# Attention with a feed-forward block: the last pass's token tiles are normalised on VectorE instead of GpSimd, and two of its operand chunks get earlier due times

## The chip, the cores and the metric

The kernel runs on one core of a Trainium2 chip. The metric is the device time of one execution in microseconds (us); three runs of the kernel before gave 906.70, 906.96 and 907.29, so the median is 906.96. In the texts TensorE is also called PE, VectorE DVE, ScalarE ACT and GpSimd POOL; SP issues the DMAs.

## The reference

Four batches, 12 heads, 448 positions, head size 64, all float32. After attention the heads are put side by side (1792 tokens of 768 features), normalised over the features, and sent through a two-layer block without a residual of the normalised value:

```
scores = cap * tanh(scale * q @ k.T / cap)
attn   = softmax(scores)                 # with + 1e-9 under the sum
x      = (attn @ v), heads side by side  # 4 x 448 x 768
mu, var = mean and variance of x over the 768 features
xn  = (x - mu) / sqrt(var + 1e-6) * g_ln
out = x + relu(xn @ w_ch1) @ w_ch2       # 768 -> 3072 -> 768
```

## The kernel before

**Tiling.** The 1792 tokens are 14 tiles of 128 (x(0) to x(13)). They are handled in four groups (GROUPS): A0 (tiles 0 to 2), A1 (3 to 5), C0 (6 to 9) and C1 (10 to 13). The 3072 hidden features are 24 blocks of 128 (FC); each block has a slice of w1 and a slice of w2. Every product is made in float32 precision from operands split into a high and a low part, as three matmuls (high by high, high by low, low by high). The split is one ACT instruction that rounds (helper `round`, L398) and one DVE instruction that takes the rest (helper `rest`, L405).

**Stages.** Attention comes first, four heads at a time (`quad`), with the group A work woven between. For A0 and A1 the FFN goes block by block (`ffn`): `up` (L883 to L885) makes the hidden values of a block in a PSUM bank, `bend` (L894 on ACT, L896 on DVE) applies relu and splits them, `down` (L912 to L914) multiplies with w2 into another bank, and a DVE add (L917) takes that bank into x. `up` and `down` share the eight PSUM banks with all else, and a bank is used again only when what it held has been read.

**The last pass.** C0 and C1 are handled last, 512 tokens each, with a seven-product scheme over 2 x 2 blocks (`last`, `stage`; matmuls L1048 to L1051). `blocks` (L927 on) prepares its operands, while the `up` and `down` work of A0 and A1 still runs. It loads the eight tiles of C0 and C1 (SP, `load_x`, L993), computes mean and reciprocal deviation in `mv` (`statistics`: DVE, with one power on POOL, L737), and normalises each tile in place, `x = (x - mean) * rstd` (L939, one instruction per tile of 128 x 768). Then, for each of KH = 3 feature chunks c, it transposes four 512-column pieces on PE (L959, four transposes of 128 x 128 in a row, one from each tile of the group), copies them out on ACT with the gain (L963, to a buffer y), forms three differences on DVE (L972) and splits the seven operands X (L398 on ACT, L405 on DVE, 128 x 512). A transpose of the group C0 needs tiles 6 to 9, one of C1 tiles 10 to 13; the instructions of PE stand in a fixed order, so a transpose that waits holds all that follows it.

**Order.** The order of each engine is made before the run by a planner (`Order.emit`): it plays the program in time with a cost for each operation and, when an engine is free, takes the ready operation that is due first. The costs are formulas: `POOL1(DM) + 61` (1006 for a tile) for L939 on POOL, `VEC1(DM) + 61` (697) for the same form on DVE in `norm` (L756). The due time of chunk c is `begin + c * PLAN["chunk"]`. The chip then runs each engine's list in that order, each instruction waiting for its semaphores.

Of the kernel before, what the change touches and what calls it, by code (L numbers as in the profile page):

```python
# [18 lines left out]
DM, DFF = H * D, 4 * H * D  # L19
# [20 lines left out]
VEC1 = lambda n: 60 + 0.75 * n  # L40
# [3 lines left out]
POOL1 = lambda n: 100 + 1.1 * n  # L44
# [27 lines left out]
PLAN = dict(  # L72
    qk=8000, pre=16000, pv=-2000, fin=9000, early=26000, start=108000, step=16700, spread=0.85, late=18,
    w1=20000, w2=3000, evac=2000, bstep=6300, cstep=31200, cnorm=10000, load=20000, zpad=3000, rush=30000, ahead=20000,
    again=12000, down=16000, chunk=12000, blocks=-30000,
)

KINDS = dict(
# [5 lines left out]
    e=('e', 3), ot=('b', 4), ss=('b', 1), stage=('a', 3),  # L84
# [9 lines left out]
    e=('e', 2), t=('e', 2), ot=('b', 3), ss=('b', 1), stage=('a', 1),  # L94
# [31 lines left out]
class Order:  # L126
# [8 lines left out]
    def add(self, engines, fn, reads=(), writes=(), allocs=(), due=0.0, dma=0, after=()):  # L135
        op = Op()
        (op.engine, op.cost), = engines.items()
        op.fn, op.due, op.dma, op.seq = fn, due, dma, len(self.ops)
        deps = set(after)
        for k in reads:  # L140
            deps.update(self.writer.get(k, ()))
        for k in writes:
            deps.update(self.writer.get(k, ()))
            deps.update(self.readers.get(k, ()))
        for k in writes:
            self.writer[k], self.readers[k] = [op], []
        for k in reads:
            self.readers.setdefault(k, []).append(op)
        deps.discard(op)
        op.left, op.outs, op.ready, op.end, op.wait, op.after = len(deps), [], 0.0, None, None, deps  # L150
        for d in deps:
            d.outs.append(op)
        bufs = {k[0] if isinstance(k, tuple) else k: 0 for k in (*reads, *writes, *allocs)}
        op.bufs = [b for b in bufs if isinstance(b, Buf)]
        for b in op.bufs:
            b.users += 1
            op.ready = max(op.ready, b.since)
        self.ops.append(op)
        return op
# [168 lines left out]
class Program:  # L328
# [25 lines left out]
    def buf(self, pool, tag, shape, dtype, bufs=1):  # L354
        size = 1
        for x in shape[1:]:
            size *= x
        kinds, tags = (GENERAL_KINDS, GENERAL_TAGS) if self.general else (KINDS, TAGS)
        if tag in tags:
            kind, n = tags[tag]  # L360
            self.limits[pool, tag] = n
            bufs, size = kinds[kind]
        else:
            kind = tag
        self.places[pool, kind] = bufs
        b = Buf(pool, kind, tag, shape, dtype)
        self.sizes[pool, kind] = max(size, self.sizes.get((pool, kind), 0))
        return b
# [558 lines left out]
    def blocks(self, due):  # L927

        nc, add, buf = self.nc, self.add, self.buf
        mvs = []
        for key in ("C0", "C1"):
            t0, nt = GROUPS[key]
            for tl in range(t0, t0 + nt):
                self.load_x(tl, due, [self.gate])
            mv = self.statistics(key, due)
            for m, tl in enumerate(range(t0, t0 + nt)):
                add({"G": POOL1(DM) + 61}, lambda e, tl=tl, mv=mv, m=m: nc.gpsimd.tensor_scalar(  # L939
                    self.x(tl), self.x(tl), mv.ap[:, m, 0:1], mv.ap[:, m, 2:3], op0=ALU.subtract, op1=ALU.mult),  # L940
                    reads=[mv], writes=[self.xkey(tl)], due=due)
        T = self.T = {}
        for c in range(KH):
            for n, name in enumerate(("11", "22", "3", "1", "2", "21", "4")):
                home = "xo1" if 7 * c + n < EARLIER else "xo2"
                T[name, c] = buf(home, f"X{name}{c}", [128, 2, TOK], F32R, 1)
        begin = due
        for c in range(KH):
            due = begin + c * PLAN["chunk"]

            def turned(y, j, n, more=(), after=()):
                key = ("C0", "C1")[n]
                t0, nt = GROUPS[key]
                ps = buf("ps", "tp", [128, 512], F32)
                k = j * KH + c

                def turn(e):
                    for m in range(nt):
                        nc.tensor.transpose(ps.ap[:, m * 128:(m + 1) * 128], self.x(t0 + m)[:, k * 128:(k + 1) * 128], self.ident)  # L959

                first = add({"T": 109 * nt}, turn, reads=[self.xkey(t0 + m) for m in range(nt)], writes=[ps],
                            allocs=[y, *more], due=due, after=after)
                add({"A": ACTP(TOK) + 93}, lambda e: nc.scalar.activation(y.ap, ps.ap, AF.Copy, scale=self.gt[:, k:k + 1]),  # L963
                    reads=[ps], writes=[y], due=due)
                return first

            def keep(name, y):
                t = T[name, c]
                self.split(Part(t, 0), Part(t, 1), y, due, n=TOK)

            def less(out, a, b):
                add({"V": VEC2(TOK)}, lambda e: nc.vector.tensor_tensor(out=out.ap, in0=a.ap, in1=b.ap, op=ALU.subtract),  # L972
                    reads=[a, b], writes=[out], due=due)

            b11, b12, b22, t3, b21 = (buf("y", "y", [128, TOK], F32) for _ in range(5))
            first = [turned(b11, 0, 0, (b12, b22, t3))]
            keep("11", b11)
            turned(b12, 0, 1, after=first)
            turned(b22, 1, 1, after=first)
            keep("22", b22)  # L980
            less(t3, b22, b12)
            keep("3", t3)
            less(b12, b12, b11)
            keep("1", b12)
            less(b22, b22, b12)
            keep("2", b22)
            turned(b21, 1, 0, after=first)
            keep("21", b21)
            less(b21, b21, b22)
            keep("4", b21)  # L990
# [256 lines left out]
```

## Time and profile before

| | us |
|---|---|
| median of three runs | 906.96 (906.70 to 907.29) |
| the profiled execution | 906.14 |
| its span, first to last instruction | 904.3 |
| PE busy | 880.2 (97% of the span) |
| DVE busy | 628.1 (69%) |
| ACT busy | 405.3 (45%) |
| POOL busy | 102.6 (11%) |
| DMA share (16 engines) | 41.9% on the main queue |

The profile is one execution recorded by the hardware. "Busy" is the time an engine spends in instructions; what is left on PE is waits. 906.14 is 1.84 above the span, for what lies around the first and last instruction. A row of the timeline shows start, length, engine, line, operation, output and input, and in brackets the idle time ahead of it with what ended it. The granted clock is the share of full speed that TensorE's throttle allowed.

### The profile page before, as it was taken

How to read it: one execution, taken by the hardware profiler on the slowest of the kernel's cores; microseconds unless marked ns; L12 is line 12 of the kernel's file. 1: busy time of each engine (PE TensorE's matmuls, PEld its weight loads, DVE VectorE, ACT ScalarE, POOL GpSimd, SP SyncE). 2: the span in 40 equal slices, each digit the busy share in tenths (PEclk: the TensorE clock that was granted, in tenths of full speed). 3: DMA queues.
4: the chain of work that ended last, by engine and by line, in shares of the span. 5: the costliest groups of instructions: out<-in, count | busy, mean ns of one | idle time of the engine just before them, and what ended most of it. 6: DMA issues, size and time to landing. Idle time of an engine off the chain costs nothing.

```text
span 904.3 us, 12584 instructions
## 1 busy us (share of the span) xinstructions
PE 880.2 (97%) x4802; PEld 727.0 (80%) x4802; DVE 628.1 (69%) x1056; ACT 405.3 (45%) x630; POOL 102.6 (11%) x122
## 2 busy tenths in 40 slices
PE   9899999999999999999969999999999999999997
PEld 4334577969878888797959889988998999899887
DVE  2995687868887777768729967665666666566544
ACT  7889746463565464643225633233223223312310
POOL 1430131111120111101380000000000000000000
PEclk9999999999999999999979999999999999999999
DMA  9995436585675655545713173111211212120004
GB/s 228 258 252 152 128 117 189 160 254 160 198 216 179 196 154 201 165 137 158 269 49 138 56 278 90 50 56 50 70 36 36 71 36 70 36 70 18 1 1 144
DMA packets 43478, 115.90 MB, mean 128 GB/s; under 512 B 6033, under 2 KB 18833, under 8 KB 43409
## 3 DMA queue, kind: packets, MB, share of 16 engines
q1 hardware_dynamic: 43408, 115.00, 41.9%
q8 instruction: 40, 0.66, 0.3%
q14 instruction: 30, 0.24, 0.1%
HBM read 87.46 MB, written 27.53 MB: 127 GB/s over the span
## 4 chain that ended last, share of the span: by engine, by line
PE 89%; DVE 3%; POOL 3%; ACT 2%; DMA 1%; issue 1%; POOLq 0%; SPq 0%; DVEq 0%; ACTq 0%
PE bank L912 13%; PE bank L914 12%; PE bank L913 12%; PE bank L1048 7%; PE bank L1051 6%; PE bank L1049 6%; PE bank L604 5%; PE bank L883 5%; PE bank L450 5%; PE bank L885 5%; PE bank L884 5%; POOL x L939 2%; PE bank L532 1%; PE bank L572 1%; PE bank L620 1%; PE bank L457 1%
## 5 line engine op out<-in xcount | busy, mean ns | idle before, releaser
L917 DVE TENSOR_TENSOR x<-bank,x 128x384 f32<-128x384 f32 x336 | 182.5, 552 | 76.7 <-PE bank L914 76.0
L912 PE MATMUL bank<-w,hh 128*128 128x384 f32 x672 | 227.9, 339 | 0.0
L914 PE MATMUL bank<-w,hl 128*128 128x384 f32 x672 | 226.8, 338 | 0.0
L913 PE MATMUL bank<-w,hh 128*128 128x384 f32 x672 | 226.8, 338 | 0.0
L912 PEld LDWEIGHTS bank<-w,hh 128*128 128x128 f32 x672 | 126.6, 188 | 5.9 <-issue 2.7
L913 PEld LDWEIGHTS bank<-w,hh 128*128 128x128 f32 x672 | 126.6, 188 | 0.6
L914 PEld LDWEIGHTS bank<-w,hl 128*128 128x128 f32 x672 | 126.6, 188 | 0.0
L1048 PE MATMUL bank<-X,q 128*128 128x512 f32 x252 | 99.7, 396 | 1.4 <-ACT y L1058 1.4
L883 PE MATMUL bank<-hA,q 128*128 128x384 f32 x288 | 100.7, 350 | 0.1
L1049 PE MATMUL bank<-X,q 128*128 128x512 f32 x252 | 99.6, 395 | 0.0
L1051 PE MATMUL bank<-X,q 128*128 128x512 f32 x252 | 99.6, 395 | 0.0
L885 PE MATMUL bank<-hA,q 128*128 128x384 f32 x288 | 98.1, 341 | 1.1 <-DVE q L405 1.1
L884 PE MATMUL bank<-lA,q 128*128 128x384 f32 x288 | 98.2, 341 | 0.0
L638 ACT ACTIVATE e<-bank,sc 128x448 f32<-128x448 f32 x144 | 81.8, 662 | 27.5 <-PE bank L604 27.4
L398 ACT ACTIVATE w<-c 128x768 fp32r<-128x768 f32 x35 | 29.0, 843 | 122.3 <-issue 78.4
L814 POOL TENSOR_SCALAR raw<-raw 128x768 f32<-128x768 f32 x48 | 51.3, 1071 | 230.2 <-ACT c L810 221.2
L405 DVE TENSOR_TENSOR q<-c,q 128x384 fp32r<-128x384 f32 (+1 forms) x88 | 60.3, 687 | 21.2 <-ACT q L398 20.6
L896 DVE SCALAR_TENSOR_TENSOR hl<-bank,hh 128x384 fp32r<-128x384 f32 (+1 forms) x60 | 34.7, 579 | 52.2 <-ACT hh L894 52.0
L398 ACT ACTIVATE q<-c 128x384 fp32r<-128x384 f32 (+1 forms) x84 | 50.2, 604 | 46.0 <-DVE c L819 16.2
L642 ACT ACTIVATE e<-e,capt 128x1344 f32<-128x1344 f32 x48 | 66.6, 1454 | 0.0
L604 PE MATMUL bank<-d 64*128 64x448 f32 x288 | 65.2, 564 | 0.6 <-DVE x L582 0.4
L894 ACT ACTIVATE hh<-bank 128x384 fp32r<-128x384 f32 (+1 forms) x60 | 30.7, 512 | 77.0 <-PE bank L885 60.7
(103 smaller groups left out, 1144.3 us busy)
## 6 DMA issues: line engine op xcount, KB each, us to landing
raw<-in_w_dram SPq DMA_DIRECT2D x48, 768.0 KB, 5.0
kept<-c SPq DMA_DIRECT2D x47, 384.0 KB, 5.6
c<-kept SPq DMA_DIRECT2D x29, 384.0 KB, 3.8
d<-in_kq_dram SPq DMA_DIRECT2D x48, 224.0 KB, 6.3
d<-kept SPq DMA_DIRECT2D x27, 384.0 KB, 3.6
x<-xd SPq DMA_DIRECT2D x16, 384.0 KB, 6.3
v<-in_v_dram SPq DMA_DIRECT2D x24, 227.5 KB, 5.3
out_dram<-x SPq DMA_DIRECT2D x28, 192.0 KB, 1.9
```

The source lines that it names most:

```text
L604: self.nc.tensor.matmul(z[k].ap[:, :S], lhsT=kqs[p].ap[rows[k], l, 128 * j:128 * j + 128], rhs=kqs[p].ap[rows[k], r], start=True, stop=True)
L638: add({"A": ACTP(S) + 93}, lambda e: nc.scalar.activation(tiles[p].ap[:, k, j] if p < 2 else er.ap[:, k], z.ap[:, :S], AF.Tanh, scale=self ...
L883: nc.tensor.matmul(ps.ap[:, :n], lhsT=w1h.ap[:, wc], rhs=xh.ap[:, c], start=(c == 0), stop=False)
L884: nc.tensor.matmul(ps.ap[:, :n], lhsT=w1h.ap[:, wc], rhs=xl.ap[:, c], start=False, stop=False)
L885: nc.tensor.matmul(ps.ap[:, :n], lhsT=w1l.ap[:, wc], rhs=xh.ap[:, c], start=False, stop=(c == CC - 1))
L912: nc.tensor.matmul(o, lhsT=h[0].ap[:, mc], rhs=w[0].ap[:, hc], start=(f == 0), stop=False)
L913: nc.tensor.matmul(o, lhsT=h[0].ap[:, mc], rhs=w[1].ap[:, hc], start=False, stop=False)
L914: nc.tensor.matmul(o, lhsT=h[1].ap[:, mc], rhs=w[0].ap[:, hc], start=False, stop=(f == last))
L917: add({"V": VEC2(HALF)}, lambda e, t=t, ps=ps, hc=hc: nc.vector.tensor_tensor(out=self.x(t)[:, hc], in0=ps.ap[:, :HALF], in1=self.x(t)[:, ...
L1048: nc.tensor.matmul(ps.ap, lhsT=wh.ap[:, wc], rhs=xs[c].ap[:, 0], start=start and c == 0, **o)
L1049: nc.tensor.matmul(ps.ap, lhsT=wh.ap[:, wc], rhs=xs[c].ap[:, 1], start=False, **o)
L1051: nc.tensor.matmul(ps.ap, lhsT=wl.ap[:, wc], rhs=xs[c].ap[:, 0], start=False, **o)
```

## The change

Two lines differ. The eight in-place normalisations of `blocks` (L939) are given to DVE, with the cost formula that `norm` uses; and PLAN["chunk"] goes from 12000 to 8000, so chunk 1 is due 4000 and chunk 2 is due 8000 planner units sooner.

```
-    again=12000, down=16000, chunk=12000, blocks=-30000,
+    again=12000, down=16000, chunk=8000, blocks=-30000,
...
-                add({"G": POOL1(DM) + 61}, lambda e, tl=tl, mv=mv, m=m: nc.gpsimd.tensor_scalar(
+                add({"V": VEC1(DM) + 61}, lambda e, tl=tl, mv=mv, m=m: nc.vector.tensor_scalar(
                     self.x(tl), self.x(tl), mv.ap[:, m, 0:1], mv.ap[:, m, 2:3], op0=ALU.subtract, op1=ALU.mult),
```

On DVE, where the statistics of C1 have just ended (L733), the eight normalisations are set between evictions of `down` banks (L917), the last steps of a weight conversion (L819, L405) and the relu rests (L896). mv_651 is the statistics tile of C0, mv_989 that of C1, x_3532 the tile that holds C0 and C1, x_433 and x_418 those of A1 and A0.

```order
 L917 TENSOR_TENSOR x_433<-bank_275,x_433 128x384
+L819 SCALAR_TENSOR_TENSOR d_75<-d_75,raw_272 128x768
 L917 TENSOR_TENSOR x_433<-bank_254,x_433 128x384
+L939 TENSOR_SCALAR x_3532<-x_3532,mv_651 128x768
+L939 TENSOR_SCALAR x_3532<-x_3532,mv_989 128x768
 L405 TENSOR_TENSOR w_69<-d_75,w_69 128x768
+L939 TENSOR_SCALAR x_3532<-x_3532,mv_989 128x768
 L896 SCALAR_TENSOR_TENSOR hl_979<-bank_264,hh_978 128x384
+L939 TENSOR_SCALAR x_3532<-x_3532,mv_989 128x768
 L896 SCALAR_TENSOR_TENSOR hl_1085<-bank_274,hh_1084 128x384
+L939 TENSOR_SCALAR x_3532<-x_3532,mv_989 128x768
 L405 TENSOR_TENSOR q_66<-d_72,q_65 128x768
```

The first three passes stand ahead of this piece, between the `down` evictions; the last two stand behind two relu rests (L896), and L819 has moved three evictions back.

On DVE some 20 instructions later, where chunks 1 and 2 are made, the differences (L972) and the rests of the operands X (L405) of chunk 1 stand among the `down` evictions (L917):

```order
 L917 TENSOR_TENSOR x_418<-bank_274,x_418 128x384
-L917 TENSOR_TENSOR x_418<-bank_281,x_418 128x384
 L972 TENSOR_TENSOR y_3682<-y_3681,y_3680 128x512
 L917 TENSOR_TENSOR x_418<-bank_253,x_418 128x384
 L405 TENSOR_TENSOR X_3841<-y_3681,X_3841 128x512
+L405 TENSOR_TENSOR X_3851<-y_3682,X_3851 128x512
+L972 TENSOR_TENSOR y_3680<-y_3680,y_3683 128x512
+L917 TENSOR_TENSOR x_418<-bank_281,x_418 128x384
+L972 TENSOR_TENSOR y_3681<-y_3681,y_3680 128x512
+L405 TENSOR_TENSOR X_3871<-y_3680,X_3871 128x512
 L917 TENSOR_TENSOR x_433<-bank_280,x_433 128x384
```

Two differences and two rests come ahead of evictions that they followed before.

On PE, at chunk 2, the order around its last transposes (L959) and the `up` matmuls (L883 to L885) between them. Before:

```order
L885 MATMUL bank_280<-hA_1053,q_68 128x384
L959 MATMUL bank_254<-ident,x_3532 128x128 x4
L959 MATMUL bank_274<-ident,x_3532 128x128 x4
L883 MATMUL bank_280<-hA_1053,q_67 128x384
L884 MATMUL bank_280<-lA_1073,q_67 128x384
...
L885 MATMUL bank_280<-hA_1053,q_68 128x384
L883 MATMUL bank_264<-hA_1053,q_65 128x384
```

And of the changed kernel:

```order
L885 MATMUL bank_280<-hA_1053,q_68 128x384
L959 MATMUL bank_264<-ident,x_3532 128x128 x4
L883 MATMUL bank_280<-hA_1053,q_67 128x384
L884 MATMUL bank_280<-lA_1073,q_67 128x384
...
L885 MATMUL bank_280<-hA_1053,q_68 128x384
L959 MATMUL bank_265<-ident,x_3532 128x128 x4
L883 MATMUL bank_274<-hA_1053,q_65 128x384
```

The last of the twelve groups of transposes goes six `up` matmuls later; all other PE instructions keep their places, with other bank numbers. On POOL the eight instructions are gone and nothing else moves; SP's order is the same.

## Rows read from the trace of the kernel before

**Rows 1.** The page's busy times: us, share of span, instructions.

```profile
PE 880.2 (97%) x4802; PEld 727.0 (80%) x4802; DVE 628.1 (69%) x1056; ACT 405.3 (45%) x630; POOL 102.6 (11%) x122
```

**Rows 2.** PE's waits from 440 to 545 us: total, times, longest.

```profile
PE bank L959 <- POOL x L939: 8.9, 4, 3.1
PE bank L885 <- DVE q L405: 1.1, 1, 1.1
PE bank L1048 <- ACT y L1058: 0.7, 1, 0.7
```

**Rows 3.** PE's timeline around the transposes and the later wait: start, us.

```profile
457.56 0.34 PE L885 MATMUL bank<-hA,q 128*128 128x384 f32 x1
...
459.19 0.77 PE L959 MATMUL bank<-ident,x 128*128 128x128 f32 x5 [0.96 <-POOL x L939]
...
462.10 0.33 PE L959 MATMUL bank<-ident,x 128*128 128x128 f32 x1
...
471.35 1.33 PE L959 MATMUL bank<-ident,x 128*128 128x128 f32 x5 [2.43 <-POOL x L939]
...
505.13 0.45 PE L885 MATMUL bank<-hA,q 128*128 128x384 f32 x1 [1.08 <-DVE q L405]
...
508.05 0.34 PE L912 MATMUL bank<-w,hh 128*128 128x384 f32 x1
```

**Rows 4.** POOL's timeline, the eight normalisations as one run.

```profile
446.88 24.41 POOL L939 TENSOR_SCALAR x<-x,mv 128x768 f32<-128x768 f32 x8
```

**Rows 5.** The form on POOL and on DVE: ns min/median/max, first and last start.

```profile
L939 POOL TENSOR_SCALAR x<-x,mv x8: 2920/2926/3504, 446.9 to 468.4; 128x768 f32<-128x768 f32 x8
...
L756 DVE TENSOR_SCALAR xn<-x,mv x6: 675/675/679, 68.4 to 113.2; 128x768 f32<-128x768 f32 x6
```

**Rows 6.** The chain's pieces, 470 to 485: start, us to the next.

```profile
472.68 0.32 PE bank L883
...
474.92 0.32 PE bank L884
...
475.43 0.18 PE bank L883
...
481.79 0.87 PE bank L959 x8
```

**Rows 7.** Busy us by stretch: PE, PEld, DVE, ACT, POOL; then PEclk, DMA.

```profile
465.00:470.00 5.00, 0.95 (x2) 0.36 (x2) 0.00 (x0) 0.00 (x0) 5.00 (x3) 0.50 0.00 0
470.00:475.00 5.00, 3.65 (x13) 3.65 (x14) 0.69 (x1) 1.74 (x3) 1.30 (x1) 0.50 0.00 0
...
459.10:473.40 14.30, 6.22 (x28) 5.12 (x29) 2.96 (x3) 3.79 (x7) 12.20 (x5) 0.70 0.11 29
473.40:504.10 30.70, 30.65 (x182) 30.18 (x181) 27.20 (x46) 19.61 (x35) 0.00 (x0) 0.97 0.34 116
```

**Rows 8.** DVE's timeline at the places the change touches: start, us.

```profile
448.66 0.95 DVE L819 SCALAR_TENSOR_TENSOR d<-d,raw 128x768 int32<-128x768 int32 x1
449.53 2.61 DVE L917 TENSOR_TENSOR x<-bank,x 128x384 f32<-128x384 f32 x5
452.46 0.96 DVE L405 TENSOR_TENSOR w<-d,w 128x768 fp32r<-128x768 f32 x1 [0.32 <-ACT w L398]
...
458.52 0.56 DVE L896 SCALAR_TENSOR_TENSOR hl<-bank,hh 128x384 fp32r<-128x384 f32 x1 [2.68 <-ACT hh L894]
...
473.44 0.69 DVE L972 TENSOR_TENSOR y<-y,y 128x512 f32<-128x512 f32 x1 [10.75 <-ACT y L963]
...
504.12 0.95 DVE L405 TENSOR_TENSOR q<-d,q 128x768 fp32r<-128x768 f32 x1
...
507.06 0.55 DVE L896 SCALAR_TENSOR_TENSOR hl<-bank,hh 128x384 fp32r<-128x384 f32 x1
```

**Rows 9.** The eight loads of tiles 6 to 13: issue times, then time to landing.

```profile
L993 SPq DMA_DIRECT2D x<-xd x8: 319/455/659, 440.5 to 443.9; - x8
...
DMA to landing us min/median/max: 4.0/7.0/8.7
```

## The prediction

> **What bounds the kernel now.** I read the page's busy times first: PE works 97% of the span, DVE 69%, POOL 11% [rows 1]. A change on DVE and POOL can therefore pay only where PE waits for them. PE's list of waits for the stretch in which L939 runs shows one large item: 8.9 us, in four waits, for L939 on POOL; then 1.1 for a weight rest on DVE and 0.7 for ACT [rows 2]. PE's own timeline shows the place: it comes to the transposes of C0 at 457.9 (457.56 + 0.34), waits 0.96 for C0's last tile, does twelve `up` matmuls, comes to C1's transposes at 462.10, and then takes one transpose per tile as POOL delivers it; the last starts at 471.35 [rows 3]. POOL runs its eight passes without a gap from 446.88 to 471.29 [rows 4], 2.93 us each [rows 5], so those four waits are POOL's pace and nothing else. The stretch table shows a second cost: from 465 to 475 the granted clock is 0.50, the 1.2 GHz level, after PE had been idle most of the way from 462 [rows 7], and the `up` matmuls from 472.68 to 475.24 go in steps of 0.32 instead of 0.18 [rows 6].
>
> **The change, part by part.** The profiled execution (906.14 us) is 0.82 below the median of 906.96; I work on its times and add 0.8 at the end.
>
> *What a pass costs on DVE.* The same form, 128x768 float32 with two per-partition scalars, stands at L756 on DVE: 0.675 us against 2.926 [rows 5]. I take 0.675; eight are 5.4 us of DVE time in place of 24.41 of POOL time. The Trainium skill ("Perfetto Trace Analysis", section "Optimizing Scalar/DVE Operations") warns against this very move: GpSimd and VectorE share an SBUF read port, so shifting work between them may not help. By it the eight passes would still fill some 24 us and end near 471.3, and the sum would be zero. The rows speak against it: in 465 to 470 DVE has no instruction at all [rows 7] and POOL's passes still take 2.93, so their length is POOL's own.
>
> *When the tiles are ready.* DVE is in order, so I add up its queue from 448.66, where L819 stood and pass 1 stands now [rows 8]. Passes 1 to 4 (2.70), the five evictions between them (2.61) and L819 (0.95) end at 454.9; C0's transposes want these four tiles at 457.9, 3.0 later. Pass 5, the rest of w (0.96) and pass 6 reach 457.2, the next relu rest (0.56) and pass 7 458.5. Pass 8 stands behind the relu rest that starts at 458.52 [rows 8], which waits for ACT and, behind it, for PE's `up` matmuls, none of which the change touches; so it starts at 459.1 and ends at 459.8. The moved edits cost DVE's queue a delay of up to 3.5 for L819 and the w rest behind it; these feed `down` matmuls that PE reaches after the transposes, so I cost them at nothing. Their cover is these 12 us or more; without it each us is a us of PE. The loads bound it from the other side: the last is issued at 443.9 and lands 8.7 later, at 452.6, the first at 444.5 [rows 9], ahead of the passes that read them.
>
> *PE without the stall.* From 457.90: eight transposes 0.87 (the undisturbed run at 481.79), twelve `up` matmuls at 0.18, 2.16, eight more transposes 0.87 [rows 6]. C1's transposes then start at 460.93, 1.2 after pass 8, and end at 461.80 instead of 472.68: 10.88 gained. PE keeps the full clock, so the eight steps from 472.68 to 475.24 give back 8 x 0.14 = 1.12 [rows 6]. Together 12.0.
>
> *What is late next.* The next wait is at 505.13, where PE waited 1.08 for the rest q_68 that DVE ended at 505.07 (504.12 + 0.95) [rows 3, 8]. Without waits PE would now be there at 505.13 - 1.08 - 12.0 = 492.05. DVE restarts its chain with the first difference (L972), 0.76 after the transposes end (473.44 against 472.68), so DVE moves by 10.88, and one rest of X fewer stands ahead of q_68 (0.69, by the 512-wide row at 473.44): 493.5 if all else repeats. In those 30.70 us DVE was idle for 3.5 [rows 7]; if all of that closes, q_68 is there at 490.0. Ends: PE goes on between 492.05 and 493.6. I take 492.5: DVE's idle is mostly waiting for ACT, which waits for PE, and PE comes 1.12 sooner relative to DVE. Gain so far 505.13 - 492.5 = 12.6. Behind it the relu rest that ended at 507.61 [rows 8], 2.54 after q_68, now has the delayed X rest ahead of it, 3.23; PE needs it 2.92 after it goes on (508.05 against 505.13) [rows 3]: about 0.25 lost. Net 12.4.
>
> *The earlier due times.* They only reorder DVE and ACT among `down` evictions and move one group of transposes six matmuls back; no instruction is added. Four operations of 0.69 come ahead of evictions, which holds PSUM banks up to 2.8 longer. I cost it at nothing, since PE fills several other banks before it comes back to one; the bound the other way is 2.8 (rival one). What follows is in the same order on every engine and moves as one; the 0.7 for ACT stays [rows 2]. The DMAs are triggered by these engines, and their share was 0.11 and 0.34 in these stretches [rows 7], so they move too.
>
> Sum: 906.14 - 12.4 = 893.7, and with 0.8 for the median 894.6 us.
>
> **Rivals.** *One: DVE is the new bound.* It was busy for 27.2 of the 30.7 us that follow the stall [rows 7]. If a `down` or `up` waits the full 2.8 for an eviction that now stands behind chunk 1's work, and q_68 comes at its late end (1.1 later than I take), 3.9 of the gain is lost: 8.5 gained, 898.5. For it: DVE has little slack, and PE arrives sooner than DVE. Against: eight banks rotate, and no wait of PE for an eviction (L917) stands in the list [rows 2].
>
> *Two: the wait only changes its name.* If the passes on DVE were late for another reason (the loads, the relu rests ahead of passes 7 and 8, the shared port above), the transposes would go on at about 471 and the kernel stays at 907. Against: 452.6 for the loads and 459.8 for pass 8 leave 1.2 us even at the tightest place; each us beyond costs one.
>
> *Three, slower: a pass costs on DVE what it costs on POOL.* Then DVE's queue from 448.66 holds eight passes of 2.926, 23.4, and 5.6 of other work ahead of pass 8 (2.61 + 0.95 + 0.96 + 2 x 0.56): it ends at 477.7, 6.4 after POOL's end, and the kernel takes 913.4. It decides from a pass of 2.1 us on, where (471.29 - 448.66 - 5.64) / 8 is used up. For it: in place, on another tile, the form is not in the trace on DVE. Against: 0.675 in all six passes of L756, with a spread of 4 ns [rows 5].
>
> **How the numbers follow.** Forecast 0.73; rival one 0.19; two 0.04; three 0.04. The forecast's own range is 893.4 (PE goes on at 492.05 and nothing is lost behind, 13.1 gained, less 0.5 for the spread of the runs) to 896.0 (493.6 and 0.25 lost, 11.3 gained, and 0.3 of spread). To leave out no more than 2 in 10 I go to rival one's price: 893.3 to 898.8. About 0.2%, 1.8 us, is what a measurement can tell from no change. Faster 0.92, within 0.04, slower 0.04.
>
> **What would show it.** Right: L939 on DVE at 0.67 to 0.70; no wait of PE for L939; PE's transposes of C1 as one run near 461; granted clock 1.00 from 465 to 475; POOL empty after 447; the wait for q_68 below 2 us, 12 to 13 us earlier. Rival one would show as PE waiting for L917 or for an X or q rest between 470 and 500. The forecast is wrong if PE waits more than 1 us at C1's transposes, if passes of L939 take 2 us, or if the stretch from 462 to 500 has new waits of more than 3 us in sum.

## The result, and the profile after

The changed kernel takes **894.58 us** (median of four executions, 893.94 to 894.83) against 906.83 for the kernel before beside it (four, 906.09 to 907.29): ratio 0.9865, 95% interval 0.9848 to 0.9882, a gain of 12.2 us. Forecast were 894.6 us and a range of 893.3 to 898.8. The profiled execution took 893.94, its span is 891.8.

The page's busy times of the kernel after: us, share of the span, instructions.

```profile
PE 877.2 (98%) x4802; PEld 725.2 (81%) x4802; DVE 631.0 (71%) x1064; ACT 405.2 (45%) x630; POOL 77.3 (9%) x114
```

Against [rows 1], DVE has eight instructions more and 2.9 us more of busy time, POOL eight fewer and 25.3 us less. PE executes the same 4802 instructions; its busy time is 3.0 us less, because fewer of them run at the lower clock and no transpose stands alone in a row of its own any more (0.33 us for one [rows 3]; below, eight together take 1.04). What PE waited for from 440 to 545 us in the kernel after (us in total, times, longest):

```profile
PE bank L1048 <- ACT y L1058: 0.7, 1, 0.7
PE bank L885 <- DVE q L405: 0.5, 1, 0.5
```

The item of 8.9 us for L939 [rows 2] is gone, no new one has come, and the wait for the weight rest q_68 has shrunk from 1.1 to 0.5. The form itself, now on DVE (ns min/median/max, first and last start):

```profile
L939 DVE TENSOR_SCALAR x<-x,mv x8: 669/671/675, 448.2 to 459.1; 128x768 f32<-128x768 f32 x8
```

0.671 us, where L756 took 0.675 and POOL 2.926 [rows 5]. DVE's timeline after, in which the passes stand (start, us; in brackets the idle time ahead):

```profile
453.13 1.26 DVE L939 TENSOR_SCALAR x<-x,mv 128x768 f32<-128x768 f32 x2
...
456.24 0.67 DVE L939 TENSOR_SCALAR x<-x,mv 128x768 f32<-128x768 f32 x1
458.60 0.56 DVE L896 SCALAR_TENSOR_TENSOR hl<-bank,hh 128x384 fp32r<-128x384 f32 x1 [1.69 <-ACT hh L894]
459.07 0.67 DVE L939 TENSOR_SCALAR x<-x,mv 128x768 f32<-128x768 f32 x1
...
462.75 0.69 DVE L972 TENSOR_TENSOR y<-y,y 128x512 f32<-128x512 f32 x1 [0.45 <-ACT y L963]
...
491.53 0.95 DVE L405 TENSOR_TENSOR q<-d,q 128x768 fp32r<-128x768 f32 x1
...
495.07 0.55 DVE L896 SCALAR_TENSOR_TENSOR hl<-bank,hh 128x384 fp32r<-128x384 f32 x1
```

The row at 453.13 holds passes 4 and 5. The fourth, C0's last, ends at about 453.8 (453.13 + 0.67); the eighth stands behind the relu rest (L896) that the forecast put ahead of it, and ends at 459.74. PE's timeline after, at the transposes, at the wait for q_68 and where the last pass's own matmuls begin:

```profile
457.82 1.04 PE L959 MATMUL bank<-ident,x 128*128 128x128 f32 x8
...
460.81 1.04 PE L959 MATMUL bank<-ident,x 128*128 128x128 f32 x8
461.60 0.42 PE L883 MATMUL bank<-hA,q 128*128 128x384 f32 x1
...
492.53 0.44 PE L885 MATMUL bank<-hA,q 128*128 128x384 f32 x1 [0.48 <-DVE q L405]
...
495.46 0.34 PE L912 MATMUL bank<-w,hh 128*128 128x384 f32 x1
495.64 0.34 PE L913 MATMUL bank<-w,hh 128*128 128x384 f32 x1
495.82 0.34 PE L914 MATMUL bank<-w,hl 128*128 128x384 f32 x1
...
501.82 0.39 PE L1048 MATMUL bank<-X,q 128*128 128x512 f32 x1
```

Where [rows 3] has transposes that come one by one until 471.35, there are now two runs of eight with no idle time in brackets. PE gets to C0's transposes at nearly the same time as before (457.82 against 457.74), so what it gains lies behind them. The stretches that answer to [rows 7] (busy us of PE, PEld, DVE, ACT, POOL; PEclk, the granted clock; DMA share, GB/s):

```profile
459.10:473.40 14.30, 14.30 (x92) 14.19 (x91) 12.62 (x22) 10.93 (x21) 0.00 (x0) 1.00 0.25 80
465.00:470.00 5.00, 5.00 (x32) 4.97 (x31) 4.93 (x10) 2.78 (x5) 0.00 (x0) 1.00 0.00 0
470.00:475.00 5.00, 5.00 (x36) 4.97 (x34) 4.26 (x9) 4.60 (x8) 0.00 (x0) 1.00 0.57 197
462.75:491.53 28.78, 28.78 (x177) 28.57 (x177) 26.71 (x46) 19.01 (x33) 0.00 (x0) 1.00 0.36 127
```

The granted clock is 1.00, the 2.4 GHz level, where it was 0.50. The last row runs from DVE's first difference (L972) to the start of the rest q_68, as the last of [rows 7] does within 0.04 us: DVE is busy for 26.71 of 28.78 us, before for 27.20 of 30.70. It is tighter, and PE waits 0.48 for it at the end.

**A yardstick in the trace.** Executions of one kernel differ by 1 us and more, which hides small terms. The stretch from PE's first transpose of C0 to its first matmul of the last pass (L1048) holds everything that the change touches and none of what comes before. In the kernel before it runs between the first and the last of these rows of PE's timeline (the middle one is the first matmul behind C1's transposes):

```profile
457.74 0.49 PE L959 MATMUL bank<-ident,x 128*128 128x128 f32 x3
...
472.33 0.67 PE L883 MATMUL bank<-hA,q 128*128 128x384 f32 x1
...
514.41 0.39 PE L1048 MATMUL bank<-X,q 128*128 128x512 f32 x1
```

That is 56.67 us; in the kernel after it is 501.82 - 457.82 = 44.00, 12.67 less. Below, this length is given for every run as "the stretch", from the same two marks in its own trace.

### The profile page after: what moved, and what is told of

It is laid out like the page before. It is cut to its first block, busy times and chain, and to the rows that moved or that the text cites. A ratio compares the mean times of both kernels' runs of the same rounds, so it can differ in the third digit from the quotient of the medians.

```text
span 891.8 us, 12568 instructions
## 1 busy us (share of the span) xinstructions
PE 877.2 (98%) x4802; PEld 725.2 (81%) x4802; DVE 631.0 (71%) x1064; ACT 405.2 (45%) x630; POOL 77.3 (9%) x114
## 4 chain that ended last, share of the span: by engine, by line
PE 91%; DVE 3%; DMA 2%; ACT 1%; issue 1%; POOL 1%; SPq 0%; DVEq 0%; ACTq 0%; POOLq 0%
PE bank L912 13%; PE bank L913 13%; PE bank L914 13%; PE bank L1048 7%; PE bank L1051 7%; PE bank L1049 7%; PE bank L883 6%; PE bank L885 5%; PE bank L884 5%; PE bank L604 5%; PE bank L450 5%; PE bank L572 1%; PE bank L532 1%; PE bank L457 1%; PE bank L620 1%; DMA raw<-in_w_dram 1%
## 5 line engine op out<-in xcount | busy, mean ns | idle before, releaser
L917 DVE TENSOR_TENSOR x<-bank,x 128x384 f32<-128x384 f32 x336 | 182.6, 553 | 76.0 <-PE bank L914 75.2
L912 PE MATMUL bank<-w,hh 128*128 128x384 f32 x672 | 227.6, 339 | 0.0
L914 PE MATMUL bank<-w,hl 128*128 128x384 f32 x672 | 226.5, 337 | 0.0
L912 PEld LDWEIGHTS bank<-w,hh 128*128 128x128 f32 x672 | 126.3, 188 | 5.9 <-issue 2.7
L914 PEld LDWEIGHTS bank<-w,hl 128*128 128x128 f32 x672 | 126.3, 188 | 0.0
L1048 PE MATMUL bank<-X,q 128*128 128x512 f32 x252 | 99.6, 395 | 1.4 <-ACT y L1058 1.4
L883 PE MATMUL bank<-hA,q 128*128 128x384 f32 x288 | 100.1, 348 | 0.1
L885 PE MATMUL bank<-hA,q 128*128 128x384 f32 x288 | 97.6, 339 | 0.5 <-DVE q L405 0.5
L405 DVE TENSOR_TENSOR q<-c,q 128x384 fp32r<-128x384 f32 (+1 forms) x88 | 60.4, 688 | 21.0 <-ACT q L398 20.0
L896 DVE SCALAR_TENSOR_TENSOR hl<-bank,hh 128x384 fp32r<-128x384 f32 (+1 forms) x60 | 34.7, 580 | 47.9 <-ACT hh L894 47.7
```

What stands on the lines that cost most here:

```text
L883: nc.tensor.matmul(ps.ap[:, :n], lhsT=w1h.ap[:, wc], rhs=xh.ap[:, c], start=(c == 0), stop=False)
L885: nc.tensor.matmul(ps.ap[:, :n], lhsT=w1l.ap[:, wc], rhs=xh.ap[:, c], start=False, stop=(c == CC - 1))
L912: nc.tensor.matmul(o, lhsT=h[0].ap[:, mc], rhs=w[0].ap[:, hc], start=(f == 0), stop=False)
L914: nc.tensor.matmul(o, lhsT=h[1].ap[:, mc], rhs=w[0].ap[:, hc], start=False, stop=(f == last))
L917: add({"V": VEC2(HALF)}, lambda e, t=t, ps=ps, hc=hc: nc.vector.tensor_tensor(out=self.x(t)[:, hc], in0=ps.ap[:, :HALF], in1=self.x(t)[:, ...
L1048: nc.tensor.matmul(ps.ap, lhsT=wh.ap[:, wc], rhs=xs[c].ap[:, 0], start=start and c == 0, **o)
```

## The experiments

Lines are those of each kernel; where code was added they are a few higher than in the kernel before (L959, the transposes, is L960 to L963, and L939 is L940 or L941). Differences in the stretch below some 0.1 us mean nothing; three kernels whose PE order and waits are alike gave 44.60, 44.59 and 44.60. Where the clock falls within the stretch it repeats less well (run 2: 0.45).

**1 and 2. The two parts alone.** First the move to VectorE with the old due times, then the earlier due times with GpSimd kept.

```
e_engine_only (from the kernel after):    chunk=8000  ->  chunk=12000
e_chunk_only  (from the kernel before):   chunk=12000 ->  chunk=8000
```

> The normalisations on VectorE, the chunk due times as before. My theory (the gain is PE's 8.9 us of waits for L939 plus some 2 us of half clock; the due times only touch the last few tenths): no wait of PE for L939, granted clock 1.00 from 465 to 475, and the wait for the rest q_68 near 505 of before stays at 0.5 to 1.6 us, because one more rest of X stands ahead of it; 894.6 to 895.8 us. Rival (the earlier due times carry a good part, by letting DVE fill its idle time): 897 us or more, with new waits of PE between 465 and 495.

Measured: 894.69 us (894.27 to 895.36), ratio 0.9867 (0.9852 to 0.9882). The stretch is 502.99 - 458.39 = 44.60. PE's waits from 440 to 545 us in this kernel:

```profile
PE bank L885 <- DVE q L405: 1.1, 1, 1.1
PE bank L1048 <- ACT y L1058: 0.7, 1, 0.7
```

> The normalisations on GpSimd as before, the chunk due times of the changed kernel. My theory: the four waits for L939 stay at 8.9 us and the half clock from 465 to 475 stays; only the 1.1 us wait for q_68 can shrink: 906.0 to 907.0 us, no difference that can be told from none beyond 0.1%. Rival (due times carry a good part): 904 us or less.

Measured: 906.52 us (905.28 to 907.04), ratio 0.9994 (0.9984 to 1.0003). The stretch is 514.07 - 458.45 = 55.62. PE's waits in this kernel:

```profile
PE bank L959 <- POOL x L939: 9.1, 4, 3.1
PE bank L1048 <- ACT y L1058: 0.7, 1, 0.7
PE bank L885 <- DVE q L405: 0.5, 1, 0.5
```

The move alone carries 56.67 - 44.60 = 12.07 of the 12.67; the due times add the other 0.60, and the wait rows show where: the wait for q_68 goes from 1.1 to 0.5 with them, on either engine. In the median that is 0.1 (894.69 against 894.58), less than its spread. With GpSimd kept, the due times leave the wait for L939 as it is (9.1), so they are no remedy for it. The stretch of that run is 1.05 under the kernel before, 0.45 more than the 0.60; this is the clock, which was lower for less long:

```profile
465.00:470.00 5.00, 0.80 (x2) 0.32 (x2) 0.00 (x0) 0.00 (x0) 5.00 (x3) 0.80 0.00 0
470.00:475.00 5.00, 2.94 (x12) 2.94 (x13) 0.69 (x1) 1.37 (x2) 2.01 (x1) 0.52 0.00 0
```

Where [rows 7] has 0.50 it is 0.80 in 465 to 470, and PE's `up` matmuls behind the transposes are slow for 1.95 us (473.04 to 474.99) in place of 2.94 (472.33 to 475.27). Whether the due times did that, or it differs from execution to execution, no run here shows.

**3. Is half of the clock a cost of its own?** The forecast counted the half-speed steps behind the wait as a term. Here GpSimd keeps the work, but PE gets something to do in the wait: dummy transposes.

```
                     for m in range(nt):
+                        for _ in range(20 * (fill and m > 0)):       # fill: C1, chunk 0
+                            nc.tensor.transpose(ps.ap[:, m * 128:(m + 1) * 128], self.x(NA)[...], self.ident)
                         nc.tensor.transpose(ps.ap[:, m * 128:(m + 1) * 128], self.x(t0 + m)[...], self.ident)
```

> The kernel before, with 20 more transposes of a tile that is already normalised put ahead of the transposes of each of the second, third and fourth tile of the second 512 tokens (the tiles that PE waits for); their results are overwritten by the transposes that follow, so the output is the same. PE then works through most of the wait on GpSimd instead of standing still, and the end of the transposes stays where GpSimd's passes put it. My theory (of the gain, about 10.9 us are the wait and about 1.1 us the half-speed steps behind it): the granted clock in 465 to 475 is 1.00, the wait for the tiles shrinks to little, the next L885 step starts where GpSimd lets it, and the time is 904.9 to 906.1, 0.8 to 2 us under the kernel before. Rival (the clock's fall costs nothing, all of the gain is the wait): 906.6 to 907.2, as before. If the added transposes overrun the wait, the time rises above both; then the wait rows tell by how much.

Measured: 904.94 us (903.98 to 905.55, 11 executions) against 906.80, ratio 0.9978 (0.9969 to 0.9987). PE's timeline of this kernel (L960 are the dummies, L961 the transposes):

```profile
461.86 0.33 PE L961 MATMUL bank<-ident,x 128*128 128x128 f32 x1
462.03 2.35 PE L960 MATMUL bank<-ident,x 128*128 128x128 f32 x20
...
471.12 0.77 PE L961 MATMUL bank<-ident,x 128*128 128x128 f32 x5 [0.40 <-POOL x L939]
471.63 0.42 PE L883 MATMUL bank<-hA,q 128*128 128x384 f32 x1
```

And its stretches, in the columns of above:

```profile
465.00:470.00 5.00, 4.30 (x37) 4.07 (x38) 0.00 (x0) 0.00 (x0) 5.00 (x3) 1.00 0.00 0
470.00:475.00 5.00, 4.60 (x31) 4.37 (x30) 2.20 (x4) 2.80 (x5) 1.06 (x1) 1.00 0.00 0
```

The last group of transposes starts at 471.12, when POOL is done, as before (471.35); the granted clock stays at 1.00, the five last transposes take 0.51 to the next matmul, and the kernel is 1.9 us faster although PE does 60 transposes more. The stretch is 512.46 - 457.50 = 54.96, 1.71 under the kernel before. PE's waits for the tiles are 2.7 us in place of 8.9, since the dummies fill them. So of the 12.67, about 1.7 is the clock's fall in the trace of the kernel before, 0.6 the due times, and the remaining 10.4 PE held at the transposes: 8.9 counted as waits, and the rest, by difference, transposes that stand alone. The rival, that the lower clock costs nothing, is out.

**4 to 6. What makes GpSimd's pass so long?** The prediction says that its 2.93 us are "POOL's own". Three forms of the pass on GpSimd, all else as before; the first two don't normalise the tiles (they leave the mean and the deviation out, or multiply by the mean).

```
before         x, mean,  rstd          op0=subtract, op1=mult
e_pool_const   x, 0.01,  1.0           op0=subtract, op1=mult      # constants, no per-partition scalars
e_pool_mulmul  x, mean,  rstd          op0=mult,     op1=mult
e_pool_madd    x, rstd, -mean * rstd   op0=mult,     op1=add       # the same result; one tiny DVE op makes the second scalar
```

> The normalisations stay on GpSimd, in the same place of the same order as the kernel before, but with two constants in place of the per-partition mean and deviation (so the tiles are not normalised). If GpSimd's pace of 2.9 us a pass is what PE waited for, and that pace comes from the per-partition scalars (L814, the same shape with constants on GpSimd, has a mean of 1.07 us on the page): the eight passes end near 456, PE has no wait for them, and the kernel takes 894.6 to 896 us with the passes still on GpSimd. If the pace is GpSimd's for any such pass: 2.9 us each and 906.9 us. If the loads or the queues around the passes set the pace: passes of 1.1 us with gaps, and 898 us or more.

Measured: 904.21 us (903.68 to 905.47), ratio 0.9974 (0.9964 to 0.9984); the stretch 54.39. PE still waits 7.1 us for L939. The form in this kernel:

```profile
L939 POOL TENSOR_SCALAR x<-x x8: 2777/2778/2782, 446.9 to 466.1; 128x768 f32<-128x768 f32 x8
```

The per-partition scalars are worth 0.15 us of a pass, not the pass: the theory that they are its cost fell. Nearest comes the branch by which GpSimd takes 2.9 us for any such pass, and the next two runs tell against that.

> The kernel before with one operation changed: the passes stay on GpSimd with their per-partition scalars, but multiply twice instead of subtract and multiply (so the tiles are not normalised). The run with constants left the passes at 2.78 us, so the per-partition scalars are not what makes them slow. New theory: the pair of operations is (every pass of 128x768 on GpSimd that multiplies twice takes 0.83 to 0.92 us at the median, L402, L811 and L814): passes of 0.9 to 1.2 us, the last done before 457, no wait of PE for L939, 894.6 to 896.0 us with all work still on GpSimd. Rival (place or the in-place tile makes it slow, whatever the operations): 2.8 to 2.9 us a pass and 906.9 us.

Measured: 894.65 us (894.42 to 895.48), ratio 0.9866 (0.9849 to 0.9882); the stretch 44.59. The form in this kernel, per-partition scalars and all:

```profile
L939 POOL TENSOR_SCALAR x<-x,mv x8: 977/978/1688, 447.5 to 455.7; 128x768 f32<-128x768 f32 x8
```

> The kernel before, the pass still on GpSimd, but written as a multiply and an add, x * rstd + (-mean * rstd), instead of a subtract and a multiply; one more tiny VectorE instruction for each 512 tokens makes the second scalar. It computes the same output. Theory A (it is the subtract that makes GpSimd's pass long): the pass takes about 1.0 us as the multiply-multiply form did, PE does not wait for the tiles, 894.4 to 895.6. Theory B (only the multiply-multiply pair is quick on GpSimd, any pair with an add-like operation takes 2.8 to 2.9 us): the wait stays, 906.5 to 907.5.

Measured: 894.56 us (894.40 to 894.78), ratio 0.9866 (0.9851 to 0.9881); the stretch 44.60. The form in this kernel, and PE's waits:

```profile
L941 POOL TENSOR_SCALAR x<-x,mv x8: 975/980/1684, 447.3 to 455.5; 128x768 f32<-128x768 f32 x8
```

```profile
PE bank L887 <- DVE q L405: 1.1, 1, 1.1
PE bank L1050 <- ACT y L1060: 0.7, 1, 0.7
```

An addition behind the multiplication is no dearer than a second multiplication; of the forms tried, only subtract-then-multiply takes three times as long. Same engine, same tiles, per-partition scalars in all three: 0.98 against 2.93 us. The normalisation could have stayed on GpSimd, written as a multiply-add, for the same gain as moving it (44.60 with the old due times, either way). So the 2.93 us are neither POOL's speed nor its memory access, but this pair of operations on it. Whether the subtraction makes it slow, or any addition or subtraction that stands first, was not tried; why the pair is slow, no run here shows.

**7. Both engines at once.** C0's tiles stay on GpSimd (subtract-multiply), C1's go to VectorE.

```
+                on_g = tl < 10
+                add({"G": POOL1(DM) + 61} if on_g else {"V": VEC1(DM) + 61}, ... self.eng(e).tensor_scalar(
```

> C0's four tiles on GpSimd, C1's four on VectorE. My theory (each transpose waits for its own tile, nothing else): GpSimd's fourth pass ends at 458.6 to 459.2, so PE waits 0.9 to 1.0 us once, C1's tiles are in time, the clock stays at 1.00: 895.3 to 896.3 us. Rival (GpSimd and VectorE slow each other when both work): passes of L939 on VectorE of 1 us and more, the last later than 461, PE waits for C1 too: 897 us or more.

Measured: 895.44 us (895.09 to 896.03), ratio 0.9874 (0.9859 to 0.9889); the stretch 504.21 - 458.30 = 45.91. PE waits once, 1.7 us, for C0's last tile, longer than the 0.9 to 1.0 expected. The form on both engines in this kernel, and GpSimd's row:

```profile
L940 POOL TENSOR_SCALAR x<-x,mv x4: 2930/3075/3512, 447.9 to 457.2; 128x768 f32<-128x768 f32 x4
L940 DVE TENSOR_SCALAR x<-x,mv x4: 676/1226/1310, 453.9 to 459.6; 128x768 f32<-128x768 f32 x4
...
447.87 12.55 POOL L940 TENSOR_SCALAR x<-x,mv 128x768 f32<-128x768 f32 x4 [0.43 <-PE bank L914]
```

GpSimd works without a gap from 447.87 to 460.42. Of the four DVE passes that start in that time, one takes 0.68 us as before and three take 1.18 to 1.31, and GpSimd's median rises from 2.93 to 3.08. Its late start (0.43) and its longer passes make up PE's longer wait. So the rival was right that the engines slow each other, and wrong on what follows: PE does not wait for C1.

The kernel before has it too, for single DVE instructions. One weight rest, before and after (1.65 us in runs 2 and 3 too, where GpSimd has the passes, and 0.95 in run 1, where it has none):

```profile
459.25 1.65 DVE L405 TENSOR_TENSOR q<-d,q 128x768 fp32r<-128x768 f32 x1 [0.18 <-ACT q L398]
...
459.66 0.95 DVE L405 TENSOR_TENSOR q<-d,q 128x768 fp32r<-128x768 f32 x1
```

Others are not touched: the rest at 452.46 took its 0.96 with GpSimd at work [rows 8]. This is part of why DVE's busy time rose by only 2.9 us in the kernel after, though the eight passes are 5.4: with the passes gone from GpSimd, DVE is no longer slowed by them.

This is the side of the Trainium skill's warning that the prediction set aside ("Perfetto Trace Analysis", section "Optimizing Scalar/DVE Operations": the two engines share an SBUF read port, so moving work between them might not help). The rows agree with it so far as the two engines slow each other while both work, by up to 0.6 us a DVE pass in this run; that the port does it, no run here shows. It did not speak against the change, since all eight passes left GpSimd and its timeline was empty by then.

**8. The last two tiles only.** As 7, with `tl < 12`: GpSimd does six tiles, VectorE two.

> Six tiles on GpSimd, the last two on VectorE. GpSimd's sixth pass ends near 465, so PE waits about 1 us at C0 and 3 us at C1's second tile, together some 4 to 5, and is idle until about 465. If only the wait counts: 898.5 to 899.6 us. If the half clock comes with the idle stretch, as before: granted clock of 0.5 to 0.8 between 463 and 473, and 1 to 2 us more, 899.6 to 901.2 us.

Measured: 901.11 us (900.54 to 901.33), ratio 0.9933 (0.9917 to 0.9950); the stretch 509.50 - 458.37 = 51.13. PE's wait for the tiles in this kernel, GpSimd's row, and two stretches:

```profile
PE bank L960 <- POOL x L940: 4.9, 3, 2.6
...
447.51 19.46 POOL L940 TENSOR_SCALAR x<-x,mv 128x768 f32<-128x768 f32 x6
...
465.00:470.00 5.00, 2.98 (x15) 2.98 (x16) 0.69 (x1) 1.57 (x3) 1.96 (x1) 0.82 0.00 0
470.00:475.00 5.00, 5.00 (x25) 5.00 (x25) 3.78 (x7) 2.42 (x6) 0.00 (x0) 0.84 0.00 0
```

The time is the one expected if the half clock comes, and it came, for part of these stretches: `up` steps of 0.32 stand from 468.49 to 471.37, and the means are 0.82 and 0.84, a little above the 0.5 to 0.8 expected. Run 2 is the kernel to compare with, since it has the same due times: two of eight passes moved bring 55.62 - 51.13 = 4.49 there, less than the 2 x 2.93 = 5.86 of GpSimd's pace. The six passes that stay take 19.46 us, while 24.41 - 5.86 = 18.55 would be their share of [rows 4]: again GpSimd's passes are longer with DVE at work beside it.

**9 and 10. How much a pass on VectorE may cost.** The kernel after, with one or three further passes over each tile behind L940 (subtract 0, multiply by 1; the values stay).

```
+                    for _ in range(1):                      # e_dve_x4: range(3)
+                        nc.vector.tensor_scalar(self.x(tl), self.x(tl), 0.0, 1.0, op0=ALU.subtract, op1=ALU.mult)
```

> The changed kernel with a second pass (subtract 0, multiply by 1) behind each of the eight on VectorE, the order otherwise the same. By the queue of the changed kernel's trace: seven tiles cost 4.2 us more ahead of the relu rest that waits until 458.6, of which its idle 1.7 takes a part; pass 8 ends near 462.7 instead of 459.7, PE waits some 1.6 us at C1's transposes, and VectorE's chain is 2 us later: 896.2 to 897.4 us. Rival (VectorE has hidden slack and 1.2 us of margin cover it): 894.6 us. Rival (VectorE is already the bound): 4.7 us more, 899.3 us.

Measured: 895.69 us (894.84 to 896.31), ratio 0.9877 (0.9861 to 0.9894); the stretch 503.31 - 457.63 = 45.68, 1.68 over the kernel after. PE waits 1.3 us for the tiles. In the median it is 1.1 above the kernel after, 0.5 below the range expected. The stretch has what was expected: in a row of DVE's timeline the next instruction starts 1.19 us after the pass (447.96 to 449.15), where in the kernel after it is 0.59 (448.17 to 448.76), so a further pass costs 0.60. The median's shortfall lies outside the stretch, in the scatter of four executions (894.84 to 896.31). The further pass itself, with constants for scalars, lasts 0.56 us, not 0.67.

> The changed kernel with three further passes behind each of the eight on VectorE, so about 2.4 us per tile, over the 2.1 us at which the prediction has the gain used up. By the same queue: C0's tiles ready near 461, C1's near 472, so PE waits 3 and 8 us, its clock falls to half for a part of it, and VectorE's chain starts near 474 as in the kernel before: 905.5 to 908.5 us. Rival (the end of the stall is not set by VectorE's queue alone; loads or ACT hide a part): 902 us or less.

Measured: 906.87 us (905.86 to 907.94), ratio 0.9999 (0.9989 to 1.0008); the stretch 516.05 - 458.32 = 57.73, 1.06 over the kernel before. PE's wait in this kernel, and the stretch in which the clock fell:

```profile
PE bank L963 <- DVE x L942: 8.7, 4, 2.7
```

```profile
470.00:475.00 5.00, 2.64 (x10) 2.34 (x11) 4.83 (x9) 1.37 (x2) 0.00 (x0) 0.50 0.11 13
```

DVE's timeline puts a tile at 2.38 us here (L940 at 448.66, the next work at 451.04). At that price the whole gain is gone and the wait is back under DVE's name, with the same fall of the clock to 0.50. 1.06 over eight tiles is 0.13, so by the stretch, and drawing a straight line, the two kernels are level at an estimated 2.25 us a tile; rival three of the prediction had put the point at 2.1.

**11 and 12. The best version.** The multiply-add on GpSimd with the earlier due times, and the kernel after once more beside it.

```
e_madd_8000 (from e_pool_madd):   chunk=12000 -> chunk=8000
e_after_again:                    the kernel after, unchanged
```

> The multiply-add form on GpSimd together with the earlier due times (8000): the candidate for a best version, since it takes 5.4 us of passes off VectorE and leaves PE without the wait for the tiles. If VectorE's load behind the transposes still holds something back, the wait for the weight rest shrinks to at most 0.5 us and the time is 0.3 to 0.8 us under the changed kernel run beside it. Rival: VectorE's 5.4 us lay in idle time anyway, and the due times are worth nothing beyond a change of the wait's length: within 0.3 us of the changed kernel.

> The changed kernel once more, beside the candidate and the kernel before: 894.3 to 895.0.

Measured: 893.93 us (893.87 to 894.26), ratio 0.9851 (0.9834 to 0.9867), and 894.09 (893.92 to 895.02), ratio 0.9855 (0.9839 to 0.9871). Both stretches are 44.00 (502.13 - 458.13 and 502.23 - 458.23). They cannot be told apart: the passes that the first takes off VectorE lay in idle time, as its rival had it. Both beat the kernel before; neither beats the other. The kernel after came out 0.2 us under the range expected of it here.

## Why the prediction was right

- **The wait.** Forecast: L939's four waits vanish, since the tiles are ready before PE asks. Shown: no such wait after, and with the passes made shorter on GpSimd itself (runs 5 and 6) the same. The pass was forecast at 0.675 and took 0.671; passes 4 and 8 were to end at 454.9 and 459.8 and ended at 453.8 and 459.7. Pass 4 was sooner by 1.1 for two reasons: the forecast added durations, while rows that follow each other start some 0.08 sooner than the last one ends (449.69 and 450.28 for one pass); and pass 1 started at 448.17, not 448.66, since a statistics step ahead of it (L731) took 0.17 us, where beside GpSimd's first pass it had taken 0.77. L819 and the w rest behind it moved back by 3.1 and 1.9 us (to 451.80 and 454.31), within the 3.5 forecast, and nothing waited for them, as forecast.
- **PE without the stall.** Forecast: C1's transposes at 460.93 to 461.80, 12.0 gained with the full clock. Measured: 460.81 to 461.60. The clock's part was sized at 1.12, the eight `up` steps; run 3 shows 1.7, since the five transposes ahead of them ran at the lower clock too (0.98 from 471.35 to 472.33, in run 3 0.51). The forecast had that difference inside its 10.88, so the sum stood.
- **What is late next.** Forecast: PE goes on behind q_68 at 492.5, within 492.05 to 493.6. Measured: 492.53. The two reasons given were one X rest fewer ahead of it and some of DVE's idle time closing, and both came. The parts were less exact than their sum: DVE's chain restarted 10.69 sooner (473.44 - 462.75) where 10.88 was taken; the rest of X shows as the 0.6 of runs 1 and 2, where 0.69 was taken; DVE idled for 2.1 us (28.78 - 26.71) against 3.5, so 1.4 closed, where the choice of 492.5 inside its range takes 1.0 of it. That these meet within 0.03 is luck; the range is what the argument gave.
- **The step that failed, a small one: 0.25 us lost behind q_68.** The relu rest did move back, by 0.60 against the weight rest (it ends 495.62 - 492.48 = 3.14 after it, before 2.54), as forecast; but nothing waited. The forecast paired it with the first `down` matmul (L912), which reads hh. The rest hl is read by L914, third in that row by the order, at 495.82, 0.20 after it is written. The loss was 0. That PE reached L1048 12.59 earlier in the trace (514.41 - 501.82) while the execution gained 12.20 is of another kind: what lies around the span was 2.14 us (893.94 - 891.8) against 1.84, and the span began with 0.1 more ahead of the transposes. So a loss forecast and not met, and 0.3 more around the span that nobody forecast, about cancel: that 894.6 lies 0.02 from the median is luck.
- **The due times.** Costed at nothing under their own name, with a possible loss of 2.8 for evictions that now stand behind chunk 1. No wait for an eviction came in any run with the earlier due times; they bring 0.60 in the stretch. The forecast has this gain in another step: the X rest that no longer stands ahead of q_68 is their doing, since it is back with the old due times (run 1).
- **The rivals.** One (DVE becomes the bound): DVE was busy for 26.71 of 28.78 us, and PE's only wait for it there was 0.48. Two and three (the wait changes its name): made to happen in run 10, at 2.38 us a tile, three and a half times what the pass costs.
- **What the prediction took for granted.** "Their length is POOL's own" was right as far as it went, POOL being slow with DVE idle; but runs 4 to 6 show the length to belong to one pair of operations. For the forecast that made no difference. For an engineer it is the larger find: the planner's cost of 1006 ns for the pass on GpSimd fits the multiply-add (0.980 us) and is a third of what the form in the kernel takes (2.926), which is likely why the planner set PE's transposes where the tiles were not yet ready; no run changes that cost alone.

## What to carry to other kernels

When PE waits for one engine's row of equal instructions, count when each consumer asks and when each pass ends on the other engine's queue: where all are early, the whole wait goes and the idle time's half clock with it, and what is left is set by the next rest or eviction in that queue. Before moving an operation because its engine is slow, try it there in another algebraic form: a multiply-add gave here what the move gave. For terms below a microsecond, measure in the trace from the last event that the edit can't touch to the first behind it, since whole executions scatter by more.

## What the runs showed of the hardware that was not expected

- GpSimd's two-operation pass over 128x768 float32: subtract-multiply 2.93 us with per-partition scalars, 2.78 with constants; multiply-multiply 0.978 and multiply-add 0.980 with per-partition scalars. On DVE subtract-multiply takes 0.671, with constants 0.560. The four GpSimd forms and the two on DVE are all that were tried.
- DVE and GpSimd slow each other down while both work, but not in every instruction: in run 7 three of four DVE passes took 1.18 to 1.31 us and one 0.68 (0.67 alone), and GpSimd's median was 3.08 (2.93); in the kernel before one DVE rest took 1.65 (0.95 after) and another its usual 0.96.
- A wait of PE costs more than its length: 1.7 us on top of 8.9 in this kernel, at the granted clock of 0.50 behind it; with the clock back sooner, 0.45 less (run 2). 60 added transposes in the wait, which do nothing for the result, made the kernel faster by 1.9 us.
